# The tail of a fused attention and adapter kernel: who adds x to the last chunks, where the range count stands, and which queue carries the last store

## The chip, the cores and the metric

The kernel runs on one core of a Trainium2 chip. The metric is the device time of one execution in microseconds, and lower is better. Runs of the kernel before: 378.57, 376.80 and 375.92 us, median 376.8. One more execution was taken with the hardware profiler; its views are what the text quotes, in microseconds from the start of its span. The engines are called TensorE (PE; its weight loads are PEld), VectorE (DVE), ScalarE (ACT), GpSimd (POOL) and SyncE (SP, which issues most transfers).

## What is computed

Two layers behind each other. First attention of 49152 queries of width 128 (four batches of 12288) over 768 keys for each batch, which are pooled 4 x 4 from `kv` and multiplied by `w_sr`; keys and values are the same. Then, for each of the 49152 rows x, a mixture of two out of eight low-rank adapters:

```python
# attention, for each batch
kv_pool = kv.reshape(B, H // r, r, W // r, r, C).mean(axis=(2, 4))
k = v = kv_pool.reshape(B, -1, C) @ w_sr
a = softmax(q @ k.T / sqrt(C))
x = a @ v
# adapters, for each row of x
logits = x @ w_gate
topk = the two largest of 8
w = softmax(those two)
out = x + sum(w[e] * (x @ A[e]) @ B[e] for e in topk)
```

## The kernel before, in words

The 49152 rows go in 96 chunks of 512 tokens (four sub-blocks of 128 partitions, the "slots"). n is the number of the last chunk, 95. For each chunk TensorE makes the scores (L326), ScalarE their exponential (L327), TensorE the weighted values with the sum of the weights in an extra column (L338), and VectorE divides by that sum (L345 and L349, or L821 and L822 for the last two chunks), which gives x; the largest gate values are taken on VectorE (L356, L827). The gate's arithmetic runs on GpSimd (L365 to L369, or `gate_args` at L762 to L765, and `gate_w` at L775 and L776), its tanh on ScalarE (L768).

The adapters of a chunk then take these steps, each a function of the kernel: x is turned by TensorE and evicted (`turn`, L790 and L796 or L798); TensorE multiplies by all A (`hidden`, L806); VectorE multiplies by the gate (`gated`, L781); the gated rows are turned again (`turn`); TensorE multiplies by B (`up`, L486) into a PSUM bank; then x is added and the 256 KB of the chunk are stored (`put`, L505).

For the addition of x there are three ways. `add_rows` (L500): VectorE adds x to the PSUM bank and writes the output tile. `take` and `add` (L491, L495): ScalarE copies the bank into the output tile, and GpSimd, which cannot read PSUM, adds x there. `x_first` (L478): TensorE puts x into the bank by a float32 product with the identity, ahead of `up`, and ScalarE copies the sum out; no addition is left. Before the change n-7, n-3 and n-1 go by VectorE, n-6, n-5 and n-4 by ScalarE and GpSimd, and n-2 by TensorE. The last chunk is split: its first two slots go by TensorE (L892, L898) and ScalarE (L900), the other two by VectorE (L904).

The kernel leaves the maximum out of its softmax, and so checks that the sums lay in a safe range. `tail_ok` compares the last 15 chunks' reciprocals with two limits on GpSimd (L571, L572) and multiplies both (L573); `all_ok` counts on TensorE by a product with ones (L577) and makes a flag on VectorE (L578, L580). All five engines load the flag (L910) and branch (L913); if it is set, the whole is computed again by a slow path, which does not happen here.

The order is written out by hand: instructions stand on each engine in the order of the code, and an engine takes them strictly one behind the other. The stores of the tail are all issued from SP, also in the order of the code. The output tiles come from a pool of three buffers with room for two chunks each; the PSUM banks of the tail are named (`bank`, `fbank`, `t_bank`, `mtile`) and reused.

Of the kernel before, what the change touches and what calls it, by code (L numbers as in the profile page):

```python
# [16 lines left out]
ALU = mybir.AluOpType  # L17
# [4 lines left out]
def kernel(  # L22
# [10 lines left out]
    nc = tc.nc  # L33
    P = 128
    B, N, C = q.tensor.shape
# [5 lines left out]
    NTOK = 512  # L41
# [27 lines left out]
    def mtile(shape, dtype=FP32, name="hd"):  # L69
        return ps_h.tile(shape, dtype, tag="hd", name=name)  # L70
# [377 lines left out]
    def as_tokens(bank):  # L448
        return bank.rearrange("p (s c) -> p s c", s=NS)
# [21 lines left out]

    dps = {}

    def x_first(c, bank):

        dps[c] = as_tokens(bank)
        for s in range(NS):
            mm(dps[c][:, s], id_f32, xn[c][:, s, 0:C], start=(s == 0), stop=False,  # L478
               skip_group_check=True)

    def up(c, bank=None):
        fresh = c not in dps
        if fresh:
            dps[c] = mtile([P, NS, P], name="d_ps") if bank is None else as_tokens(bank)
        for s in range(NS):
            mm(dps[c][:, s], columns(hgT[c], c, s), b_bf, start=(s == 0 and fresh),  # L486
               stop=(s == NS - 1), skip_group_check=True)

    def take(c, lo=0, hi=NS):
        osb = half_out()  # L490
        nc.scalar.activation(osb[:, lo:hi], dps[c][:, lo:hi], AF.Copy)  # L491
        return osb

    def add(c, osb, eng):
        eng.tensor_tensor(osb, osb, xn[c][:, :, 0:C], op=ALU.add)  # L495

    def add_rows(c, lo=0, hi=NS, osb=None, bank_=None):
        osb = half_out() if osb is None else osb
        d = dps[c][:, lo:hi] if bank_ is None else bank_
        nc.vector.tensor_tensor(osb[:, lo:hi], d, xn[c][:, lo:hi, 0:C], op=ALU.add)  # L500
        return osb

    def put(c, osb, lo=0, hi=NS, queue=None):
        t0 = c * NTOK
        (queue or nc.sync).dma_start(  # L505
            out[t0:t0 + NTOK, :].rearrange("(p s) c -> p s c", p=P)[:, lo:hi], osb[:, lo:hi])
# [63 lines left out]
    def tail_ok():  # L570
        nc.gpsimd.tensor_scalar(ok[:, tail], rv[:, tail], 1.0 / L_HI, None, op0=ALU.is_ge)  # L571
        nc.gpsimd.tensor_scalar(low, rv[:, tail], 1.0 / L_LO, None, op0=ALU.is_le)  # L572
        nc.gpsimd.tensor_tensor(low, low, ok[:, tail], op=ALU.mult)  # L573

    def all_ok(bank):
        n = (NCH - CUT) * NS
        mm(bank[0:1, 0:n], ones_c, low, start=True, stop=True)  # L577
        nc.vector.tensor_reduce(last, bank[0:1, 0:n], axis=AX.X, op=ALU.add)  # L578
        full = float(P * NCH * NS + P * 2 * B + 2 * B)
        nc.vector.tensor_scalar(bad, last, tot, full, op0=ALU.add, op1=ALU.not_equal)  # L580


# [171 lines left out]
    def bank(i):  # L754
        return ps_e.tile([P, NTOK], FP32, tag=f"e{i}", name=f"e{i}")
# [22 lines left out]
    def gated(c, lo, hi, g, hb):  # L778
        if c not in hg:
            new_hg(c)  # L780
        nc.vector.tensor_tensor(  # L781
            hg[c][:, lo:hi].rearrange("p s (r e) -> p s r e", e=E),
            hb.rearrange("p s (r e) -> p s r e", e=E),
            g[:, lo:hi].unsqueeze(2).broadcast_to([P, hi - lo, RK, E]), op=ALU.mult)

    def turn(src, lo, hi, bank_, store, key, act=True):

        t_ps = bank_.bitcast(BF16)[:, 0:(hi - lo) * P].rearrange("p (s c) -> p s c", c=P)
        for s in range(lo, hi):
            mm(t_ps[:, s - lo], src[:, s], id_bf, is_transpose=True,  # L790
               start=(s == lo), stop=(s == hi - 1), skip_group_check=True)
        if key not in store:
            x_or_h = ("xt", 7) if store is xT else ("ht", 4)
            store[key] = run.tile([P, NS, P], BF16, tag=x_or_h[0], name="xr", bufs=x_or_h[1])
        if act:
            nc.scalar.activation(store[key][:, lo:hi], t_ps, AF.Copy)  # L796
        else:
            nc.vector.tensor_copy(store[key][:, lo:hi], t_ps)  # L798

    def high(c):  # L800
        return xn[c].bitcast(U16)[:, :, 1:2 * C:2].bitcast(BF16)
# [16 lines left out]
    def tops4(c, top, y):  # L818
        ri = rinv_all[:, c]
        xv = y[:, :, 0:2 * VW].rearrange("p b (s v) -> p b s v", v=VW)  # L820
        nc.vector.reciprocal(ri.rearrange("p (b s) -> p b s", b=2), xv[:, :, :, VW - 1])  # L821
        nc.vector.tensor_tensor(  # L822
            xn[c][:, :, 0:C + G].rearrange("p (b s) v -> p b s v", b=2), xv[:, :, :, 0:C + G],
            ri.rearrange("p (b s) -> p b s", b=2).unsqueeze(3).broadcast_to([P, 2, 2, C + G]),
            op=ALU.mult)
        for s in range(NS):
            nc.vector.max(top[:, s], xn[c][:, s, C:C + E])  # L827
# [13 lines left out]
    def fbank(i):  # L841
        return ps_f.tile([P, NTOK], FP32, tag=f"f{i}", name=f"f{i}")
# [6 lines left out]
    o6 = take(n - 6)  # L849
    h2 = hidden(n - 3, 0, NS, mtile([P, NTOK], name="h2"))  # L850
    up(n - 5, bank(0))
    o0 = take(n - 5)
    gate_args(n - 1, 0, NS, nc.gpsimd, top4, arg4, msk4)
    y5 = ps_e.tile([P, 2, 512], FP32, tag="y5", name="y5")
    weigh(n, 0, y5)
    gated(n - 3, 0, NS, gw[q_ - 1][:, 0:NS], h2)
    turn(high(n - 1), 0, NS, bank(1), xT, n - 1)
    h3 = hidden(n - 2, 0, NS, t_bank())
    gated(n - 2, 0, NS, gw[q_ - 1][:, NS:2 * NS], h3)
# [3 lines left out]
    o1 = take(n - 4)  # L863
    gate_w(0, NS, nc.gpsimd, arg4, msk4)
    tops4(n, top5, y5)
    turn(hg[n - 3], 0, NS, mtile([P, NTOK], name="t2"), hgT, n - 3)
    h4 = hidden(n - 1, 0, NS, bank(1))
    turn(hg[n - 2], 0, NS, t_bank(), hgT, n - 2)
    x_first(n - 2, fbank(0))
    turn(high(n), 0, NS, bank(0), xT, n)  # L870
    add(n - 6, o6, nc.gpsimd)
    put(n - 6, o6)
    gate_args(n, 0, NS, nc.gpsimd, top5, arg5, msk5)
    gate_tanh(0, NS, arg5)
    up(n - 3, mtile([P, NTOK], name="d2"))
    gated(n - 1, 0, NS, arg4, h4)
    put(n - 3, add_rows(n - 3))
    up(n - 2)
    o3 = take(n - 2)
    gate_w(0, NS, nc.gpsimd, arg5, msk5)  # L880
    x3 = ps_e.tile([P, 2, 512], FP32, tag="y5", name="x3")
    h5 = hidden(n, 0, NS, x3[:, 0])
    gated(n, 0, NS, arg5, h5)
    put(n - 2, o3)
    for c, o in ((n - 5, o0), (n - 4, o1)):
        add(c, o, nc.gpsimd)
        put(c, o)
    tail_ok()
    turn(hg[n - 1], 0, NS, bank(1), hgT, n - 1)
    d5 = as_tokens(fbank(1))  # L890
    for s in range(2):
        mm(d5[:, s], id_f32, xn[n][:, s, 0:C], start=(s == 0), stop=False, skip_group_check=True)  # L892
    turn(hg[n], 0, 2, bank(0), hgT, n)
    turn(hg[n], 2, 4, t_bank(), hgT, n, False)
    up(n - 1, mtile([P, NTOK], name="d4"))
    put(n - 1, add_rows(n - 1))
    for s in range(2):
        mm(d5[:, s], hgT[n][:, s], b_bf, start=False, stop=(s == 1), skip_group_check=True)  # L898
    o5 = half_out()
    nc.scalar.activation(o5[:, 0:2], d5[:, 0:2], AF.Copy)  # L900
    d6 = as_tokens(fbank(0))
    for s in range(2, 4):
        mm(d6[:, s - 2], hgT[n][:, s], b_bf, start=(s == 2), stop=(s == 3), skip_group_check=True)
    nc.vector.tensor_tensor(o5[:, 2:4], d6[:, 0:2], xn[n][:, 2:4, 0:C], op=ALU.add)  # L904
    put(n, o5)
    all_ok(bank(1))

    end_banks.close()
    ps_g = ctx.enter_context(tc.tile_pool(name="ps_g", bufs=1, space=bass.MemoryType.PSUM))
# [124 lines left out]
```

## Time and profile before

| what | us |
|---|---|
| median of three runs | 376.8 |
| the profiled execution, its own time | 375.43 |
| its span | 373.6 |
| TensorE busy | 356.5 |
| ScalarE busy | 309.4 |
| VectorE busy | 299.6 |
| GpSimd busy | 225.6 |
| last exponential ends on ScalarE | about 354 |
| the flag is written on VectorE | 370.14 |

How to read the lines of the prediction: a row of the timeline gives start, length, engine and line, the operation, what is written and read, the shapes, and in brackets the engine's idle time ahead of it with what ended it. A row of the chain gives start, length and what, of the one chain of work that ended last. In the strip of the DMA engines each digit is the busy share of a slice in tenths; the strip has 40 slices of the stretch named ahead of it.

### The profile page before, as it was taken

The page shows a single profiled execution, that of the slowest core. Times are in us where ns is not written, and L with a number is a line of the kernel's source. Part 1 is how long each engine was busy: PE and PEld are TensorE (multiplying, and loading weights), DVE is VectorE, ACT ScalarE, POOL GpSimd, SP SyncE. Part 2 cuts the span into 40 slices and gives each one's busy share as a digit, 9 for nine tenths or more (in the row PEclk, how much of TensorE's full clock was granted, in tenths as well). Part 3 has the DMA queues.
Part 4 walks back from the last instruction along what each step waited for, and adds up shares of the span by engine and source line. Part 5 has one row for each costly group of instructions (what it writes and reads, how often), then busy time and mean ns, then how long its engine had stood idle before and what let it go on. Part 6 is the DMA issues. An engine that isn't in the chain of part 4 may idle for free.

```text
span 373.6 us, 10589 instructions
## 1 busy us (share of the span) xinstructions
PE 356.5 (95%) x3942; PEld 262.8 (70%) x3943; DVE 299.6 (80%) x952; ACT 309.4 (83%) x391; POOL 225.6 (60%) x376
## 2 busy tenths in 40 slices
PE   4789999999999999999999999999999999999983
PEld 2456777777777677777777777777776767667772
DVE  3784558888888788888888888888888898998983
ACT  1579999989889798898898898898888888888862
POOL 1013799988799897755679697755444234232255
PEclk9999999999999999999999999999999999999998
DMA  8998999999999999999999999998789799663325
GB/s 261 413 360 218 316 300 304 298 318 306 286 335 320 308 292 331 226 317 314 304 288 361 303 313 317 253 302 260 227 225 257 206 255 245 184 145 131 130 86 201
DMA packets 95594, 101.01 MB, mean 270 GB/s; under 512 B 58804, under 2 KB 59060, under 8 KB 95540
## 3 DMA queue, kind: packets, MB, share of 16 engines
q1 hardware_dynamic: 94068, 100.11, 94.6%
q8 instruction: 31, 0.51, 0.6%
q10 hardware_dynamic: 1472, 0.20, 0.3%
q14 instruction: 23, 0.19, 0.2%
HBM read 62.33 MB, written 25.90 MB: 236 GB/s over the span
## 4 chain that ended last, share of the span: by engine, by line
PE 83%; DVE 5%; POOL 4%; DMA 3%; ACT 2%; issue 1%; SPq 0%; POOLq 0%; DVEq 0%
PE xps L338 33%; PE sg L326 30%; PE t_ps L405 5%; PE d_ps L486 5%; PE h_ps L440 4%; DMA kvt<-in_kv_dram 2%; DMA ge<-g_h 2%; ACT tt L327 1%; PE v_ps L215 1%; POOL osb L495 1%; DVE xn_all L349 1%; DVE osb L500 1%; DVE ht L443 1%; DVE kvt L191 1%; PE k_ps L240 1%
## 5 line engine op out<-in xcount | busy, mean ns | idle before, releaser
L327 ACT ACTIVATE tt<-sg 128x1024 f16<-128x1024 f32 x288 | 276.9, 1023 | 36.3 <-PE sg L326 35.5
L326 PE MATMUL sg<-qT,kfT 128*128 128x512 f16 x576 | 170.2, 379 | 0.5 <-ACT qT L593 0.3
L338 PEld LDWEIGHTS <-tt 128*128 128x128 f16 x2304 | 146.1, 98 | 28.4 <-DVE xn_all L349 18.1
L338 PE MATMUL xps<-vext,tt 128*128 128x136 f16 x2256 | 164.7, 223 | 0.3 <-DVE xn_all L349 0.2
L500 DVE TENSOR_TENSOR osb<-d_ps,xn_all 128x512 f32<-128x512 f32 x85 | 58.7, 691 | 28.7 <-PE d_ps L486 27.7
L365 POOL TENSOR_TENSOR arg<-xn_all,top 128x64 f32<-128x64 f32 x47 | 14.5, 308 | 99.6 <-DVE top L356 80.2
L349 DVE TENSOR_TENSOR xn_all<-xps,rinv_all 128x540 f32<-128x540 f32 x94 | 67.7, 721 | 3.3
L326 PEld LDWEIGHTS <-kfT 128*128 128x128 f16 x576 | 49.1, 98 | 24.4 <-issue 1.5
L191 POOL TENSOR_TENSOR kvt<-kvt 128x1024 f32<-128x1024 f32 x27 | 63.7, 2361 | 2.1 <-PE t_ps L405 2.0
L107 POOL CAST q<-q 128x1024 f16<-128x1024 f32 x45 | 46.8, 1042 | 24.0 <-DMA q<-in_q_dram 24.0
L443 DVE SCALAR_TENSOR_TENSOR ht<-ge,h_ps 128x512 bf16<-128x512 f16 x87 | 58.5, 673 | 1.4 <-DMA ge<-g_h 1.0
L486 PEld LDWEIGHTS <-ht 128*128 128x128 bf16 x368 | 27.0, 98 | 24.6 <-DVE ht L443 5.7
L356 DVE MAX8 top<-xn_all 128x8 f32<-128x8 f32 x376 | 35.1, 156 | 6.3
L416 DVE COPY xt<-t_ps 128x512 bf16<-128x512 bf16 x92 | 36.8, 400 | 0.0
L405 PE MATMUL t_ps<-id_bf,xn_all 128*128 128x128 bf16 x376 | 36.3, 219 | 0.0
L486 PE MATMUL d_ps<-b_bf,ht 128*128 128x128 bf16 x340 | 32.9, 219 | 0.8 <-DVE ht L443 0.7
L440 PE MATMUL h_ps<-xt,a_bf 128*128 128x512 bf16 x86 | 32.6, 379 | 0.1
L345 DVE RECIPROCAL rinv_all<-xps 128x4 f32<-128x4 f32 x94 | 17.1, 182 | 13.6 <-PE xps L338 12.2
L405 PEld LDWEIGHTS <-xn_all 128*128 128x128 bf16 x376 | 25.9, 98 | 0.3
L368 POOL TENSOR_SCALAR msk<-msk 128x64 f32<-128x64 f32 x47 | 20.2, 429 | 4.1
L369 POOL TENSOR_TENSOR arg<-arg,msk 128x64 f32<-128x64 f32 x47 | 15.1, 321 | 3.9
L367 POOL TENSOR_TENSOR arg<-arg,msk 128x64 f32<-128x64 f32 x47 | 15.1, 320 | 3.7
(150 smaller groups left out, 221.0 us busy)
## 6 DMA issues: line engine op xcount, KB each, us to landing
kvt<-in_kv_dram SPq DMA_DIRECT2D x48, 512.0 KB
q<-in_q_dram SPq DMA_DIRECT2D x46, 512.0 KB
out_dram<-osb SPq DMA_DIRECT2D x44, 512.0 KB
ge<-g_h SPq DMA_DIRECT2D x45, 256.0 KB
out_dram<-osb SPq DMA_DIRECT2D x8, 256.0 KB
q<-in_q_dram SPq DMA_DIRECT2D x1, 1024.0 KB
qT<-q SPq DMA_TRANSPOSE x46
g_h<-g_sb SPq DMA_DIRECT2D x45, 16.0 KB
```

The lines of the kernel that those rows point to most:

```text
L107: nc.gpsimd.tensor_copy(q16[i], q32[i].rearrange("p k n -> p (k n)"))
L191: eng.tensor_tensor(v[:, 0], v[:, 0], v[:, d], op=ALU.add)
L326: mm(sg[:, k], kfT[b][:, j * P:(j + 1) * P], qc, start=True, stop=True)
L327: nc.scalar.activation(tt[c][:, 2 * r:2 * r + 2], sg, AF.Exp, bias=0.0, scale=scale)
L338: mm(o, tt[c][:, j, s * P:(s + 1) * P], vext[b][:, j, 0:VW], start=(j == 0 and s % 2 == 0), stop=(j == NJ - 1 and s % 2 == 1), skip_group_ ...
L349: nc.vector.tensor_tensor(xn[c][:, :, 0:C + G].rearrange("p (b s) v -> p b s v", b=2), xv[:, :, :, 0:C + G], ri.rearrange("p (b s) -> p b ...
L405: mm(columns(t_ps, c, s), src[:, s], id_bf, is_transpose=True, start=(s == 0), stop=(s == NS - 1), skip_group_check=True)
L416: nc.vector.tensor_copy(to, t_ps)
L440: mm(h_ps, a_bf, xT[c], start=True, stop=True)
L443: nc.vector.scalar_tensor_tensor(hgT[c].rearrange("p (k a) t -> p k (a t)", k=2), gE[c // 2][:, h:h + NS // 2].rearrange("p a t k -> p k ( ...
L486: mm(dps[c][:, s], columns(hgT[c], c, s), b_bf, start=(s == 0 and fresh), stop=(s == NS - 1), skip_group_check=True)
L500: nc.vector.tensor_tensor(osb[:, lo:hi], d, xn[c][:, lo:hi, 0:C], op=ALU.add)
```

## The change

All of it is in the tail, from L471 on; the loop over the chunks stays.

- n-5: VectorE adds x from PSUM (`add_rows`); ScalarE's copy and GpSimd's addition go.
- n-6: its addition on GpSimd moves ahead of the gate weights of n-1, and its store behind that of n-5.
- n-2: VectorE adds x; TensorE's eight float32 products with the identity and ScalarE's copy go.
- n-1: TensorE puts x under it (`x_first`, now callable for some slots, in two halves) and ScalarE copies; VectorE's addition goes.
- n-4: still ScalarE and GpSimd, its addition now behind the gate weights of n.
- The range tests move ahead of the gate of n, and the product of the two comparisons goes: TensorE counts both, and the expected count is larger by that number.
- Count and flag move from behind the last store to behind the last turning of n.
- The float32 products of the first half of n write another bank (the second of the tile that holds the hidden rows of n) and stand behind `up(n - 1)`.
- The last store is issued from ScalarE's queue.

```diff
-    def x_first(c, bank):
-        dps[c] = as_tokens(bank)
-        for s in range(NS):
+    def x_first(c, bank, lo, hi):
+        dps[c] = as_tokens(bank) if lo == 0 else dps[c]
+        for s in range(lo, hi):
...
     def tail_ok():
...
-        nc.gpsimd.tensor_tensor(low, low, ok[:, tail], op=ALU.mult)
...
-        mm(bank[0:1, 0:n], ones_c, low, start=True, stop=True)
+        mm(bank[0:1, 0:n], ones_c, ok[:, tail], start=True, stop=False)
+        mm(bank[0:1, 0:n], ones_c, low, start=False, stop=True)
...
-        full = float(P * NCH * NS + P * 2 * B + 2 * B)
+        full = float(P * (NCH * NS + n) + P * 2 * B + 2 * B)
...
     up(n - 5, bank(0))
-    o0 = take(n - 5)
...
     gated(n - 3, 0, NS, gw[q_ - 1][:, 0:NS], h2)
+    put(n - 5, add_rows(n - 5))
+    add(n - 6, o6, nc.gpsimd)
+    put(n - 6, o6)
...
     gate_w(0, NS, nc.gpsimd, arg4, msk4)
     tops4(n, top5, y5)
+    tail_ok()
...
     turn(hg[n - 2], 0, NS, t_bank(), hgT, n - 2)
-    x_first(n - 2, fbank(0))
     turn(high(n), 0, NS, bank(0), xT, n)
-    add(n - 6, o6, nc.gpsimd)
-    put(n - 6, o6)
...
     up(n - 3, mtile([P, NTOK], name="d2"))
+    x_first(n - 1, fbank(1), 0, 2)
     gated(n - 1, 0, NS, arg4, h4)
+    up(n - 2, fbank(0))
     put(n - 3, add_rows(n - 3))
-    up(n - 2)
-    o3 = take(n - 2)
-    gate_w(0, NS, nc.gpsimd, arg5, msk5)
+    put(n - 2, add_rows(n - 2))
     x3 = ps_e.tile([P, 2, 512], FP32, tag="y5", name="x3")
     h5 = hidden(n, 0, NS, x3[:, 0])
+    turn(hg[n - 1], 0, NS, bank(1), hgT, n - 1)
+    gate_w(0, NS, nc.gpsimd, arg5, msk5)
     gated(n, 0, NS, arg5, h5)
-    put(n - 2, o3)
-    for c, o in ((n - 5, o0), (n - 4, o1)):
-        add(c, o, nc.gpsimd)
-        put(c, o)
-    tail_ok()
-    turn(hg[n - 1], 0, NS, bank(1), hgT, n - 1)
-    d5 = as_tokens(fbank(1))
+    x_first(n - 1, fbank(1), 2, 4)
+    up(n - 1)
+    o4 = take(n - 1)
+    put(n - 1, o4)
+    add(n - 4, o1, nc.gpsimd)
+    put(n - 4, o1)
+    d5 = as_tokens(x3[:, 1])
     for s in range(2):
         mm(d5[:, s], id_f32, xn[n][:, s, 0:C], start=(s == 0), stop=False, skip_group_check=True)
     turn(hg[n], 0, 2, bank(0), hgT, n)
     turn(hg[n], 2, 4, t_bank(), hgT, n, False)
-    up(n - 1, mtile([P, NTOK], name="d4"))
-    put(n - 1, add_rows(n - 1))
+    all_ok(bank(1))
...
-    d6 = as_tokens(fbank(0))
+    d6 = as_tokens(mtile([P, NTOK], name="d6"))
...
-    put(n, o5)
-    all_ok(bank(1))
+    put(n, o5, queue=nc.scalar)
```

## The prediction

> **What bounds the kernel now.** I read the page's first part and its chain first: they say what the body is bound by, and so whether an edit of the tail can matter.
>
> ```profile
> span 373.6 us, 10589 instructions
> PE 83%; DVE 5%; POOL 4%; DMA 3%; ACT 2%; issue 1%; SPq 0%; POOLq 0%; DVEq 0%
> ```
>
> TensorE carries 83% of the chain, but the order of the changed program differs from that of the old one only after the last exponential, from about 358 us on. So the body keeps its time, and I look only at the last 15 us. There the chain in order of time is another one (columns: start, length, what):
>
> ```profile
> 362.60 0.25 POOL r L776
> 362.86 1.22 POOL osb L495
> ...
> 365.85 2.44 POOL osb L495 x2
> 368.29 0.33 POOL ok L571
> 368.62 0.33 POOL low L572
> ...
> 369.03 0.32 POOL low L573
> ...
> 369.39 0.28 PE e L577 x2
> ...
> 369.70 0.22 DVE last L578
> ...
> 369.94 0.20 DVE bad L580
> ```
>
> GpSimd ends last: behind the last gate (ending at 365.85) it adds two chunks (2.44), runs the range tests, and only then TensorE counts and VectorE writes the flag, at 370.14.
>
> What follows the flag comes from the rows of the flag's load (L910) and of the program's end (L1029):
>
> ```profile
> L910 SPq TENSOR_LOAD <-bad x1: 869/869/869, 370.2 to 370.2; - x1
> ```
>
> ```profile
> L1029 SPq EVENT_SEMAPHORE x10: 17/28/28, 372.3 to 373.6; - x10
> L1029 SPq DRAIN x3: 7/7/13, 372.8 to 373.1; - x3
> ```
>
> From the flag's end to the end of the span are 373.6 - 370.1 = 3.5 us of load, branch, semaphore checks and barrier, all fixed. SP starts its closing checks at 372.3 and runs through them without a gap. A second path ends there too, that of the stores (the SP rows, then the busy tenths of the DMA engines, the first strip from 358.75 in steps of 0.05 us, the second from 369.25 in steps of 0.1 us):
>
> ```profile
> 358.75 0.34 SPq L505 DMA_DIRECT2D out_dram<-osb  x1
> ```
>
> ```profile
> DMA  0000000000000000169898997989966300000000
> ```
>
> ```profile
> 369.28 0.37 SPq L505 DMA_DIRECT2D out_dram<-osb  x1
> ```
>
> ```profile
> DMA  9999999999999998999721000000022003000000
> ```
>
> A store that finds the DMA engines empty is moved 1.6 us after its issue (358.75 to 360.35). The last store, issued at 369.28 into a queue that is full, is mostly moved by 371.25 and has stragglers until 371.5. It is not late, but it is not far from being so: SP's checks come about 0.8 us behind it.
>
> **The change part by part.** These rows of the timeline carry the terms (start, length, engine and line; in brackets the engine's idle time before):
>
> ```profile
> 361.65 0.69 DVE L781 TENSOR_TENSOR hgs<-t_ps,th 128x512 bf16<-128x512 f32 x1 [1.00 <-PE t_ps L806]
> ...
> 362.22 0.29 POOL L775 TENSOR_SCALAR r<-r 128x32 f32<-128x32 f32 x1 [0.91 <-ACT r L768]
> ...
> 362.81 1.27 POOL L495 TENSOR_TENSOR osb<-osb,xn_all 128x512 f32<-128x512 f32 x1
> ...
> 363.05 1.11 PE L478 MATMUL f<-xn_all,id_f 128*128 128x128 f32 x8
> ...
> 363.33 0.37 DVE L827 MAX8 top<-xn_all 128x8 f32<-128x8 f32 x4
> ...
> 364.00 0.39 PE L790 MATMUL e<-id_bf,xn_all 128*128 128x128 bf16 x4
> ...
> 364.04 0.24 POOL L762 TENSOR_TENSOR r<-xn_all,top 128x32 f32<-128x32 f32 x1
> ...
> 364.65 0.69 DVE L500 TENSOR_TENSOR osb<-d,xn_all 128x512 f32<-128x512 f32 x1 [0.35 <-PE d L486]
> ...
> 365.22 0.29 POOL L775 TENSOR_SCALAR r<-r 128x32 f32<-128x32 f32 x1
> ...
> 365.53 0.66 PE L892 MATMUL f<-xn_all,id_f 128*128 128x128 f32 x4
> ...
> 365.60 0.25 POOL L776 TENSOR_TENSOR r<-r,r 128x32 f32<-128x32 f32 x1
> 365.79 0.60 ACT L796 ACTIVATE xr<-e 128x512 bf16<-128x512 bf16 x1 [0.17 <-PE e L790]
> ...
> 365.88 0.69 DVE L781 TENSOR_TENSOR hgs<-x,r 128x512 bf16<-128x512 f32 x1 [0.54 <-POOL r L776]
> ...
> 366.63 0.28 PE L790 MATMUL e<-id_bf,hgs 128*128 128x128 bf16 x2 [0.44 <-DVE hgs L781]
> ...
> 367.01 0.38 ACT L796 ACTIVATE xr<-e 128x256 bf16<-128x256 bf16 x1 [0.62 <-PE e L790]
> 367.14 0.29 DVE L798 COPY xr<-t_ps 128x256 bf16<-128x256 bf16 x1 [0.56 <-PE t_ps L790]
> ...
> 367.94 0.41 DVE L904 TENSOR_TENSOR osb<-f,xn_all 128x256 f32<-128x256 f32 x1
> ```
>
> 1. *Chunk n-5 from GpSimd to VectorE.* 0.69 us on VectorE, placed ahead of the 361.65 row, which has 1.00 idle before it: covered, cost nothing. Its ScalarE eviction goes. Were the idle time not there, the gating of n-2 and all behind it would slip by up to 0.69.
> 2. *Chunk n-6 earlier on GpSimd.* 1.27 us goes ahead of the 362.22 row, into 0.91 of idle time: the weights of n-1 come 1.27 - 0.91 = 0.36 later, at 362.85 + 0.36 = 363.21. Their reader, the gating of n-1, stands on VectorE behind the maxima of the last chunk, which end at 363.33 + 0.37 = 363.70; so the 0.36 is covered, with 0.49 to spare.
> 3. *Range tests, without the product, ahead of the gate of n.* 2 x 0.33 from the chain's rows: 363.21 + 0.66 = 363.87, against 364.04 now, because the add that stood there has gone. The last gate's weights are ready 0.17 earlier: 365.85 - 0.17 = 365.68.
> 4. *x under n-2 on TensorE goes (8 matmuls, 1.11), VectorE adds n-2 instead.* The turning of x of n at 364.00 may go up to 0.7 earlier and the product of n-3 with it, so VectorE's add of 364.65 moves to about 364.3; the new add (0.69) follows it and ends at 365.68, in the 0.54 of idle time and the 0.35 gained. Gating of n: 365.72 instead of 365.88, ending at 366.41. This cover is exact: each tenth that the add of n-3 does not gain puts the gating back by the same tenth.
> 5. *x under n-1 (two halves of 4 matmuls).* They lie where TensorE waits: ahead of the product of n-2, and behind the turning of n-1. ScalarE's eviction of that turning, now at 365.79, loses its take of n-2 ahead of it and comes near 365.4; the product of n-1 is done by 366.4. GpSimd's and VectorE's adds for it are gone; ScalarE takes 0.6 instead, before it is needed for the last turning.
> 6. *x under the first half of n.* Now 4 matmuls at 365.53, off the path. In the new order they write the second bank of the tile whose first bank the gating of n reads, and the built program lets them wait for that gating. They stand ahead of the last turning, so this is a new cost on the path: eight such took 364.00 - 363.05 = 0.95 until the next group, four 0.48. Last turning: 366.41 + 0.06 + 0.48 = 366.95 against 366.63, 0.32 later.
> 7. *Count and flag.* VectorE's copy of the turning moves by the same 0.32 and ends at 367.75. TensorE counts meanwhile (two products where the chain has one of 0.28; 367.2 to about 367.6). Sum and compare take 370.14 - 369.70 = 0.44: flag at 368.20 against 370.14, 1.94 us earlier. The product on GpSimd (0.32) is gone.
> 8. *The last store.* VectorE's last add (0.41) stands behind the flag: 368.20 to 368.62, against 368.35 now. But there the store still stood behind four others on SP until 369.28; on ScalarE's queue it issues near 368.70, 0.58 earlier. SP's seven stores go out earlier too (n-5 and n-6 by 362.7, n-3, n-2, n-1 between 365 and 367.5, n-4 when GpSimd's add ends, 365.68 + 1.27 = 366.95, behind n-1). Behind the issue on ScalarE only its own flag load is queued, so it loads about 0.9 later than SP; SP's checks come 2.1 us after its load began, which covers it.
>
> The price of a store on ScalarE's queue is not in the tail. The nearest rows are the first load there and its reader:
>
> ```profile
> 0.74 0.40 ACTq L138 DMA_DIRECT2D w_in<-in_w_sr_dram  x1
> ```
>
> ```profile
> 2.79 0.23 DVE L155 TENSOR_SCALAR w_sr_sb<-w_in 128x128 f32<-128x128 f32 x1 [1.93 <-DMA w_in<-in_w_sr_dram]
> ```
>
> Issue 0.40 against 0.34, and 2.05 us from issue to its reader for 64 KB. So the last store (256 KB) is moved 1.6 us after issue if the engines are empty, or, as the one at 369.28, in 2.3 us if they are not: 370.3 to 371.0. From the moved data to the end of the span lies at least 0.85 (SP's first closing drain at 372.8 to 373.65) and at most 2.1 (371.5 to 373.6). I take 1.3, between them and nearer the lower, since SP went through its checks unhindered: 371.6 to 372.3.
>
> **Sum.** Flag path: 368.20 + 3.5 = 371.7. Store path: 371.6 to 372.3, middle 372.0. The later decides: span 372.0, a gain of 1.6 us. The profiled execution took 375.43 us by its own time, 1.8 outside the span; it becomes 373.8. It lies 1.4 under the median of the runs (376.8), so the median becomes 375.2.
>
> By the Trainium skill ("DMA: Bandwidth & Descriptors", Anatomy of one DMA, which speaks of the GpSimd path) a transfer costs about 2.0 us fixed, most of it the receipt of the last write, plus its bytes over 436 GB/s. That makes an estimate of 2.6 us here, a landing at 371.3 and an end near 372.2, so the store and not the flag would decide; the 64 KB load (2.05 seen, 2.15 by the rule) agrees.
>
> **Rivals.**
> *The stores decide by more.* Moving the adds earlier leaves the same eight stores of 256 KB for sixteen DMA engines, and the strip shows one or two engines late (the 1, the 2 after 371.2). If one engine is a store or two behind, the last one is moved near 371.5 as now, less one store's 0.6: span 372.6 to 373.2, gain 0.4 to 1.0, median 376.1. For it: the stragglers. Against: two of the eight now leave before 363.
> *Nothing is gained.* The late turning (step 6) grows: if the add of n-2 holds the gating of n by another 0.7 and the x half by its whole 0.66, flag at 369.1 and last store at 369.6, moved by 371.9. Span 373.4, median 376.6. For it: the cover of step 4 has no reserve. Against: 365.68 on both engines.
> *Slower.* ScalarE's queue has carried nothing since the start. The second load there reached its reader later than the first:
>
> ```profile
> 1.17 0.45 ACTq L140 DMA_DIRECT2D w_gate_sb<-in_moe_w_gate_dram  x1
> ```
>
> ```profile
> 5.36 0.56 PE L165 MATMUL wg_ps<-w_gate_sb,wT 128*128 128x8 f32 x2 [1.74 <-DMA w_gate_sb<-in_moe_w_gate_dram]
> ```
>
> That is 4.19 us from issue to reader. The last store makes the kernel slower from 373.65 - 0.85 - 368.7 = 4.1 us after issue on. At 4.19 the span is 373.7; with the upper bound of what follows, 2.1 behind data moved at 372.3, it is 374.4: median 376.9 to 377.6. For it: a queue this long unused. Against: the 2.05 of the first load, on a queue equally unused, and that the second load's 4 KB go in rows of 32 bytes, which the store's do not.
> *Only the flag counts.* Store moved at 370.3 and receipt short: span 371.7 or, without step 6's wait, 371.3; median 374.5 to 374.9.
>
> **How the numbers follow.** Forecast (gain 1.2 to 2.0) 0.58, stores by more 0.18, flag alone 0.08, nothing 0.09, slower 0.07. The runs before spread from 375.92 to 378.57, and the profiled one was at 375.43; the forecast's own range is 375.43 - 2.0 = 373.4 to 376.8 - 1.2 = 375.6. With the two rivals of smaller gain, and half a microsecond for the runs, 373.5 to 377.1 holds 8 in 10. One per cent, 3.8 us, is about what a measurement of this kernel can tell from no change. No case gains that: the whole stretch from the last gate to the flag is 4.3 us, of which the turnings stay. So faster 0.04 and slower 0.03, both for the spread of the runs and the tail of the ScalarE case, same 0.93.
>
> **What would show it.** Right: GpSimd's last add ends near 367.0 with no range test behind it; the flag near 368.2; VectorE with three adds at 128x512 after 361; TensorE's last turning near 366.95 behind the four float matmuls; a store on ScalarE's queue near 368.7. Wrong: a gap of SP in its closing checks of more than 0.5 us (the store decides), the gating of n after 366.0 (step 4 or 3), the last store's data after 371.2, or a body longer than now ahead of 358 us.

## The result and the profile after

| | before | after |
|---|---|---|
| median of 20 runs, us | 375.89 (375.28 to 380.62) | 374.75 (373.77 to 376.81) |
| ratio, 95% interval | | 0.9957 [0.9940, 0.9973] |
| the profiled execution, us | 375.43 | 374.92 |
| its span | 373.6 | 373.0 |

The time falls by 1.1 us of 376, within the one per cent that the prediction called no change; it had 375.2. The first part and the chain of the page of after:

```profile
span 373.0 us, 10593 instructions
PE 84%; DMA 7%; DVE 5%; ACT 1%; issue 1%; SPq 1%; POOL 1%; ACTq 0%; DVEq 0%
```

GpSimd's share of the chain fell from 4% to 1%. The two spans can't simply be subtracted. The first store that both programs issue at the same point of the work, that of n-7, stands at 358.75 in before and here:

```profile
359.85 0.34 SPq L505 DMA_DIRECT2D out_dram<-osb  x1
```

That is 1.1 us later. It is scatter of the body: in eight profiled executions of kernels with the new tail and an untouched body (after, E1 to E4, E6, E11, E12) this store is issued between 358.63 and 359.85, and in E5, which has the body of before, at 360.13. It arises at the start. ScalarE's waits ahead of the exponentials (L327) run in before and in after

```profile
L327 ACTq EVENT_SEMAPHORE  x92: 17/17/17, 32.2 to 350.6; - x92
```

```profile
L327 ACTq EVENT_SEMAPHORE  x92: 17/17/17, 33.3 to 351.7; - x92
```

which is 318.4 us from the first to the last in both: the 1.1 us are there by the first row and do not change any more. So the tails are compared from the issue of n-7 on, and I call that time z. The tail of before lasts from 358.75 to 373.65, 14.90 us; that of after from 359.85 to 373.03, 13.18: 1.72 less, where the prediction had 1.6.

The chain of after in order of time (start, length, what):

```profile
364.46 0.40 PE e L790 x4
...
365.22 0.50 PE f L478 x4
...
366.52 0.60 ACT xr L796
367.13 0.05 issue
367.17 0.40 PE f L486 x4
367.57 0.56 PE x L894 x4
368.13 0.13 PE e L790 x2
...
368.34 0.39 ACT xr L796
...
368.78 0.29 PE x L899 x2
369.06 0.13 PE d L904 x2
...
369.21 0.42 DVE osb L905
```

The late additions and the range tests on GpSimd (L495, L571 to L573), which carried before's chain from 362.9 to 369.4, are off it; the one late addition left on GpSimd (n-4) stands beside it. The chain now runs over TensorE and ScalarE, through the product of n-1 (L486) and x of the last chunk's first half (L894), to the last turning, and ends at the addition for the last store. The waits of SP from 366 us on say which path ends last (who waits, for whom, us in total, times, longest):

```profile
SPq L505 <- DVE osb L500: 2.3, 2, 1.9
...
SPq L1029 <- DMA out_dram<-osb: 0.5, 1, 0.5
```

The second line is the answer to "which path decides": SP's closing checks (L1029) stop for half a microsecond until a store has landed. Before had no such wait. By the trace's rows it lasts 0.56 us, from 371.51 to 372.07. So the flag has half a microsecond in hand.

The timeline rows for the prediction's steps (start, length, engine and line, operation):

```profile
361.67 0.68 DVE L500 TENSOR_TENSOR osb<-e,xn_all 128x512 f32<-128x512 f32 x1
362.75 0.69 DVE L781 TENSOR_TENSOR hgs<-t_ps,th 128x512 bf16<-128x512 f32 x1 [0.41 <-PE t_ps L806]
```

```profile
363.98 0.25 POOL L776 TENSOR_TENSOR r<-r,r 128x32 f32<-128x32 f32 x1
...
364.52 0.36 POOL L572 TENSOR_SCALAR low<-rinv_all 128x60 f32<-128x60 f32 x1
364.65 0.60 ACT L796 ACTIVATE xr<-t_ps 128x512 bf16<-128x512 bf16 x1
...
365.31 0.68 DVE L500 TENSOR_TENSOR osb<-d,xn_all 128x512 f32<-128x512 f32 x1
365.98 0.69 DVE L500 TENSOR_TENSOR osb<-f,xn_all 128x512 f32<-128x512 f32 x1
...
366.39 0.25 POOL L776 TENSOR_TENSOR r<-r,r 128x32 f32<-128x32 f32 x1
...
366.60 1.26 POOL L495 TENSOR_TENSOR osb<-osb,xn_all 128x512 f32<-128x512 f32 x1
366.68 0.69 DVE L781 TENSOR_TENSOR hgs<-x,r 128x512 bf16<-128x512 f32 x1
...
367.42 0.71 PE L894 MATMUL x<-xn_all,id_f 128*128 128x128 f32 x4
...
367.97 0.27 PE L790 MATMUL e<-id_bf,hgs 128*128 128x128 bf16 x2
...
368.94 0.20 DVE L580 TENSOR_SCALAR bad<-last,tot 1x1 int32<-1x1 f32 x1
...
369.72 0.38 ACTq L505 DMA_DIRECT2D out_dram<-osb  x1
```

And the DMA engines of after, from 366 us in steps of 0.1:

```profile
DMA  0000000838899988989898601000013799999999
...
q8 instruction: 1, 0.02, 2.1%
```

There are two things here that the prediction's sum did not have. The stores of n-3 and n-2 are moved from 366.7 to 368.2, and behind them about one engine of the sixteen is still at work (digits of 0 and 1). And in the same stretch falls one 16 KB packet on queue 8: the DMA engines also bring TensorE's next instructions.

### The profile page after: what moved, and what is told of

It is laid out like the page before. It is cut to its first block, busy times and chain, and to the rows that moved or that the text cites. A ratio compares the mean times of both kernels' runs of the same rounds, so it can differ in the third digit from the quotient of the medians.

```text
span 373.0 us, 10593 instructions
## 1 busy us (share of the span) xinstructions
PE 358.1 (96%) x3945; PEld 263.0 (70%) x3945; DVE 300.2 (80%) x953; ACT 308.7 (83%) x390; POOL 223.5 (60%) x374
## 4 chain that ended last, share of the span: by engine, by line
PE 84%; DMA 7%; DVE 5%; ACT 1%; issue 1%; SPq 1%; POOL 1%; ACTq 0%; DVEq 0%
PE xps L338 34%; PE sg L326 30%; PE t_ps L405 5%; PE d_ps L486 5%; PE h_ps L440 5%; DMA b_f<-in_moe_B_dram 3%; DMA kvt<-in_kv_dram 2%; DMA ge<-g_h 2%; PE v_ps L215 1%; ACT tt L327 1%; DVE xn_all L349 1%; DVE osb L500 1%; DVE ht L443 1%; SPq L87 1%; PE kp_ps L207 0%
## 5 line engine op out<-in xcount | busy, mean ns | idle before, releaser
L327 ACT ACTIVATE tt<-sg 128x1024 f16<-128x1024 f32 x288 | 276.8, 1022 | 37.2 <-PE sg L326 36.5
L486 PEld LDWEIGHTS <-ht 128*128 128x128 bf16 x368 | 26.9, 98 | 24.8 <-DVE ht L443 6.1
L486 PE MATMUL d_ps<-b_bf,ht 128*128 128x128 bf16 x340 | 32.9, 219 | 0.7 <-DVE ht L443 0.7
```

What stands on the lines that cost most here:

```text
L327: nc.scalar.activation(tt[c][:, 2 * r:2 * r + 2], sg, AF.Exp, bias=0.0, scale=scale)
```

## The experiments

The prediction's account, theory A: the new division of the additions lets both paths to the end come forward; x of the last half waits (step 6), and the last store, not the flag, decides by a few tenths. Its rivals: one part alone (the flag, or ScalarE's queue) carries the gain; or the stores are held back by something else than their issue. The last became theory C after E4: it is the load of TensorE's instructions that makes one DMA engine late, and that engine sets the end. Each expectation states what it holds against what; that of E1 names theory C, since it was written after the results of E2 to E5.

All in us from z; each line is one profiled execution, the ratios are from 7 to 12 timed runs (after: 20) against before. "Landed" is when 15 of the 16 engines, and when the last one, reported the last store done.

| kernel | last turning | flag | last store issued | landed, 15 / 16 | end | ratio, 95% interval |
|---|---|---|---|---|---|---|
| before | 7.88 | 11.39 | 10.53 | 12.96 / 13.39 | 14.90 | |
| after | 8.12 | 9.29 | 9.87 | 11.94 / 12.21 | 13.18 | 0.9957 [0.9940, 0.9973] |
| E1 after again | 8.11 | 9.28 | 9.86 | 11.95 / 12.42 | 13.39 | |
| E2 last store on SP | 8.11 | 9.28 | 9.87 | 12.90 / 13.15 | 14.12 | 0.9953 [0.9932, 0.9975] |
| E3 flag last | 8.12 | 10.14 | 9.87 | 11.93 / 12.18 | 13.22 | 0.9959 [0.9934, 0.9985] |
| E4 x early | 7.65 | 8.82 | 9.71 | 12.50 / 12.63 | 13.61 | 0.9955 [0.9931, 0.9980] |
| E5 before, flag early | 7.87 | 9.27 | 11.15 | 14.09 / 14.55 | 15.52 | 1.0025 [0.9995, 1.0054] |
| E6 x and count aside | 7.57 | 7.86 | 9.62 | 12.79 / 12.90 | 13.87 | 0.9967 [0.9954, 0.9980] |
| E7 load moved | 8.11 | 9.28 | 9.86 | 11.94 / 12.08 | 13.05 | 0.9977 [0.9958, 0.9996] |
| E8 = E6 with E7 | 7.57 | 7.86 | 9.62 | 11.93 / 13.65 | 14.63 | 1.0021 [1.0006, 1.0036] |
| E9 load clear of all | 8.11 | 9.28 | 9.86 | 11.92 / 11.95 | 12.92 | 0.9989 [0.9965, 1.0013] |
| E10 all aside, load clear | 7.57 | 7.86 | 9.33 | 11.57 / 12.02 | 13.00 | 0.9979 [0.9955, 1.0004] |
| E11 = E10, old start | 7.57 | 7.86 | 9.33 | 12.12 / 12.24 | 13.22 | 0.9971 [0.9951, 0.9992] |
| E12 adds alone | 8.12 | 10.13 | 9.87 | 12.22 / 12.81 | 13.78 | 0.9955 [0.9939, 0.9971] |

**E1, the changed kernel again.** Nothing edited.

> The changed kernel, unaltered, profiled once more, to see how far the tail's length repeats. Theory C, formed from the runs so far (16 KB of TensorE's instructions are loaded in the midst of the last stores, by one of the sixteen DMA engines, which is then behind for all later stores, and by more or less from run to run): the engines' own steps repeat to 0.05 (last turning 8.1, flag 9.3, last store issued 9.9 after the store of n-7), while the landing of the last store and with it the tail moves by some tenths, 13.1 to 13.7. Rival (the tail repeats as a whole): 13.2, within 0.05.

The engines' steps repeat to 0.01; the landing of the last store moved by 0.2, and with it the end (13.39 against 13.18). So a difference of a step is read to hundredths, one of the end only to some tenths.

**E2, the last store on SP.**

```diff
-    put(n, o5, queue=nc.scalar)
+    put(n, o5)
```

> The changed kernel with one thing undone: the last store is issued from SP again. Measure for this and the other runs: the tail, from the issue of the store of n-7 to the end of the span (14.9 us in the kernel before, 13.2 in the changed one), because the body's own spread is larger than the effects. Theory A (the landing of the last store ends the tail, SP waits for it 0.5 us in its closing checks, the flag has that much in hand): SP's flag load starts only behind the issue, at about 0.95 later than now, uses up the 0.5 and becomes the end itself: tail 13.6, no gap left in SP's checks. Rival B (the queue does not matter, what counts is the moment VectorE's last add ends): tail 13.2.

The time does not change against after (0.9953), and neither of the two tails expected (13.6, 13.2) came: it is 14.12. SP issues the store at z + 9.87, no later than ScalarE did. In this profiled execution the stores land later, but that begins before the edited place: the third of the late stores, that of n-1, occupies SP for 0.89 us where it took 0.33 in after.

```profile
367.68 0.89 SPq L505 DMA_DIRECT2D out_dram<-osb  x1
```

Before shows such a long issue, too, at 367.10 (0.81), for its third late store, that of n-5. So ScalarE's queue brings no earlier issue; the issue came forward because SP has nothing left to wait for when VectorE's last addition is done.

**E3, the flag behind the last store again.**

```diff
-    all_ok(bank(1))
...
     put(n, o5, queue=nc.scalar)
+    all_ok(bank(1))
```

> The changed kernel with count and flag put back behind the last store; the adds and the queue stay as changed. Theory A (the store decides, the flag has 0.5 us in hand): the flag comes about 1.0 later, half of it is absorbed, tail 13.6 to 13.7. Rival B (the flag decides already in the changed kernel): the whole 1.0 is lost, tail 14.2.

The flag comes 0.85 later and the end does not move (13.22, ratio 0.9959). The half microsecond of SP's wait for the store is used up, as its waits show: there is one for the flag (L910) and none for a store any more.

```profile
SPq L910 <- DVE bad L580: 1.0, 1, 1.0
SPq L1029 <- PEq L1029: 0.6, 2, 0.5
```

I had expected the end to come some tenths later. From the flag to the end it took 3.08 us here against 3.51 in before: the stretch that the prediction called fixed is not. SP's load of the flag took 0.76 us in after and 0.48 here (0.87 in before; why it differs was not tried):

```profile
L910 SPq TENSOR_LOAD <-bad x1: 761/761/761, 369.2 to 369.2; - x1
```

```profile
L910 SPq TENSOR_LOAD <-bad x1: 480/480/480, 369.0 to 369.0; - x1
```

So of the 0.85 by which the flag is later, the load gives back 0.28, and SP's wait of 0.56 holds the rest.

**E4, x of the last half ahead of its wait.** The two products go into a bank that is free earlier, ahead of `up(n - 1)`.

```diff
+    d5 = as_tokens(fbank(0))
+    for s in range(2):
+        mm(d5[:, s], id_f32, xn[n][:, s, 0:C], start=(s == 0), stop=False, skip_group_check=True)
     up(n - 1)
...
-    d5 = as_tokens(x3[:, 1])
-    for s in range(2):
-        mm(d5[:, s], id_f32, xn[n][:, s, 0:C], start=(s == 0), stop=False, skip_group_check=True)
```

> The changed kernel, with the x of the first half of n put into the bank that n-2 has left, ahead of the product of n-1, so that it does not wait for the gating of n. Theory A (these four float32 products are a new 0.5 us on the path to the last turning, and the last store behind it ends the tail): the turning of the gated rows of n starts 0.35 after the gating ends minus what the product of n-1 takes, near 0.25 behind it instead of 0.6; everything behind moves by 0.35, tail 12.8. Rival B (TensorE waits there for the eviction of the turning of n-1 anyway, the products are hidden): tail 13.2.

The last turning is at 366.98, z + 7.65, 0.47 earlier: the wait of step 6 is real and its size right. But the end did not follow (13.61; ratio 0.9955). The last store is issued only 0.16 earlier and lands later, at 12.63, and SP waits for stores:

```profile
SPq L1029 <- DMA out_dram<-osb: 0.8, 2, 0.6
```

So here the end did not come from the turning. With all that E2 showed this led to theory C.

**E5, before with an early flag.** In before, `tail_ok()` (in its new form) goes ahead of the loop that adds n-5 and n-4, and the count behind `up(n - 1)`.

```diff
+    tail_ok()
     for c, o in ((n - 5, o0), (n - 4, o1)):
         add(c, o, nc.gpsimd)
         put(c, o)
-    tail_ok()
...
     up(n - 1, mtile([P, NTOK], name="d4"))
+    all_ok(bank(1))
...
     put(n, o5)
-    all_ok(bank(1))
```

> The kernel before with the early flag alone: range tests (two comparisons, no product) ahead of the last two adds on GpSimd, count and flag behind the last turning; who adds x to which chunk and the queue of the last store stay as before. Theory A (flag and stores are two paths that end close together): the flag comes near 368.0, but the two adds slip by 0.66, the last store is issued near 369.9 and decides: tail 14.8 to 15.0, no gain against 14.9. Rival B (the late flag alone was the loss): flag at 368.0 plus 3.5, tail 12.7.

The flag is as early as in after (9.27), and nothing is gained: tail 15.52, ratio 1.0025. The tests go ahead of GpSimd's additions, these move back, and SP waits for them in its stores; its own load of the flag stands behind them at z + 11.69, 2.4 behind the flag.

```profile
SPq L505 <- POOL osb L495: 2.4, 2, 1.6
...
SPq L1029 <- DMA out_dram<-osb: 0.5, 1, 0.5
```

An early flag is worth nothing without the new division of the additions.

**E6, x and the count aside.** The turnings of n go ahead of x of its first half, and the count goes ahead of `up(n - 1)` into a bank of its own.

```diff
+    all_ok(mtile([P, NTOK], name="cnt"))
     up(n - 1)
...
+    turn(hg[n], 0, 2, bank(0), hgT, n)
+    turn(hg[n], 2, 4, t_bank(), hgT, n, False)
     d5 = as_tokens(x3[:, 1])
...
-    turn(hg[n], 0, 2, bank(0), hgT, n)
-    turn(hg[n], 2, 4, t_bank(), hgT, n, False)
-    all_ok(bank(1))
```

> The changed kernel with two things taken out of the way of the last turning: the x of the first half of n stands behind that turning, and count and flag stand ahead of it, in a bank that is free by then. By the engines' rows the last turning comes 0.5 earlier (7.6 after the store of n-7), the flag near 8.0, the last store is issued near 9.4. If the engines' path ends the tail: 12.6 to 12.7. By theory C (the DMA engine that is behind sets the landing, whatever the engines do): the store lands no earlier than 12.2 and the tail is 13.1 or more, although its issue is 0.5 earlier.

The flag is 1.43 earlier, the turning 0.55, the last store's issue only 0.25, since ScalarE's copy of n-1 (0.60), which stood ahead of its copy of the turning before, too, now ends after the turning and holds that copy up. The end is later (13.87): again n-1's issue takes 0.88, and the stores land late. It is not one engine alone: the last store, issued 0.27 behind that of n-4, has landed on fourteen engines only at 12.32, 2.70 behind its issue, and on the other two at 12.79 and 12.90. So theory C's one late engine does not tell the whole of this run.

```profile
SPq L505 <- ACT xr L796: 1.4, 1, 1.4
SPq L1029 <- DMA out_dram<-osb: 0.9, 2, 0.6
```

**E7, the load of instructions moved.** The page of after has the loads in its part on queues (packets, MB, share):

```profile
q8 instruction: 31, 0.51, 0.6%
```

That is 16 KB each, one for some 254 of TensorE's 3945 matmuls and 3945 weight loads. A start with 124 more TensorE instructions shifts it: half of the 18 warming products (`warm`, products at the start whose result nobody reads) are replaced by 71 products of one column, whose result nobody reads either.

```diff
-    warm(18)
+    warm(9)
+    tiny = mtile([P, 1], name="tiny")
+    for i in range(71):
+        mm(tiny, id_bf, id_bf[:, 0:1], start=True, stop=True)
```

> The changed kernel; at the start, nine of the 18 warming products are replaced by 71 one-column products, so that TensorE's program is 124 instructions longer ahead of the tail and the load of its last 16 KB of instructions falls 4 to 5 us earlier, between the stores of n-7 and n-5. The start of the kernel may shift by some tenths, the tail's engines' steps do not. Theory C: no DMA engine is behind at the last store, it lands about 2.05 after its issue instead of 2.34, SP's wait shrinks from 0.56 to about 0.25, tail 12.8 to 12.9. Rival (the stragglers come from the stores' own density): 13.2.

The load went from z + 6.9 to z + 2.5. The store of n-3 now lands at 8.17 with 15 engines and 8.20 with the last (after: 8.19 and 9.72), those of n-2, n-1 and n-4 within 0.04, and the end is at 13.05 (12.8 to 12.9 expected). It is the store of n-5, the one just issued when the load starts, that now has a late engine (landed at 4.53 and 5.10). In the strip of the DMA engines (from 368 in steps of 0.1) nothing straggles behind the first pair of stores:

```profile
DMA  8899998989899610000000999899898999971399
```

That is theory C's evidence by removal. The ratio is 0.9977, no better than after's: z was at 360.99, so the altered start cost the body what the tail gained, or more.

**E8, E6 and E7 together.**

> Both: count, flag and x aside of the last turning, and the instruction load moved. Theory C with the engines' path: last store issued near 9.4, landed at 11.45; SP's flag load stands behind its own issue for n-4 and starts near 9.2; tail 12.4 to 12.6, against 13.2, and the time 0.6 us under that of the changed kernel, if the altered start costs nothing. Rival: the tail stays at 12.9 or more, because something else holds the landing.

This was meant to be the best version and became the second slowest. The four late stores ahead of the last land together. But in E7, too, a further load of 16 KB comes at the jump behind the flag, at z + 11.77, when the last store is all but landed; with the early flag TensorE jumps earlier, and the load is at z + 10.87, in the midst of that store. In both runs it starts 1.2 us behind the end of TensorE's branch (z + 10.59 and 9.64). Fifteen engines had it done at 11.93, one at 13.65, and SP waited 2.1 us for it:

```profile
SPq L1032 <- DMA out_dram<-osb: 2.1, 1, 2.1
```

```profile
DMA  9899999898999898305002000101010010000000
...
q8 instruction: 1, 0.02, 2.0%
```

The strip (from 370 in steps of 0.1) shows that one engine, its work trickling in until 373.3. That is theory C's evidence by addition: the same load behind the store's issue costs the end 1.6 us against E7, and the time shows it (1.0021).

**E9, the load clear of all late stores.** As E7, with 13 warming products and 33 of one column (56 more instructions).

> The changed kernel with five of the 18 warming products at the start replaced by 33 one-column products: TensorE's program is 56 instructions longer ahead of the tail, so the load of its last 16 KB of instructions should fall about 4.5 us after the store of n-7, between the stores of n-6 and n-3, and the next one behind the end. In the run that moved it by 124 instructions, a further load came with the jump at the end and met the last store. Theory C (the load alone makes one DMA engine late): all sixteen engines land every store from n-3 on within 0.1 us, the last store lands about 2.1 after its issue at 9.87, tail 12.9 to 13.0 against 13.2 to 13.4. Rival (the stragglers have another cause): first and last landing of the stores stay 1.5 us apart.

The load is at z + 4.2, and the late engine has gone with it: the store of n-6 lands at 5.81 with fifteen engines and at 7.12 with the last. All five late stores land on the last engine within 0.04 of the fifteenth, the last store at 11.95, 2.09 behind its issue, the shortest tail of all (12.92). In the strip from 371 nothing of the store is left behind its 3 at 373.2 (three small loads of instructions, 8 KB each, make the 5 and the 2), and SP's wait is 0.3:

```profile
DMA  8999999989999615898999305000200000000000
```

```profile
SPq L1032 <- DMA out_dram<-osb: 0.3, 1, 0.3
```

Against after's 13.18 the late engine is thus worth 0.26, against E1's 13.39 it is 0.47. The time does not show it (0.9989): z was at 361.77. The body lost that in its middle, not at its start: the waits at L327 run from 32.5 to 353.6, 321.1 us against 318.4, and over the whole run VectorE waits longer for the gate values of the chunks (`ge`) to be loaded, E9 first, then after:

```profile
DVE ht L443 <- DMA ge<-g_h: 4.1, 5, 1.7
```

```profile
DVE ht L443 <- DMA ge<-g_h: 1.1, 2, 0.9
```

**E10 and E11, all aside.** E6 with ScalarE's copy of n-1 behind the turnings of n and the store of n-4 ahead of it; E10 with E9's start, E11 with the old one.

```diff
+    all_ok(mtile([P, NTOK], name="cnt"))
     up(n - 1)
-    o4 = take(n - 1)
-    put(n - 1, o4)
     add(n - 4, o1, nc.gpsimd)
     put(n - 4, o1)
+    turn(hg[n], 0, 2, bank(0), hgT, n)
+    turn(hg[n], 2, 4, t_bank(), hgT, n, False)
+    o4 = take(n - 1)
+    put(n - 1, o4)
...
-    turn(hg[n], 0, 2, bank(0), hgT, n)
-    turn(hg[n], 2, 4, t_bank(), hgT, n, False)
-    all_ok(bank(1))
```

> The changed kernel with count, flag and x of n's first half out of the way of the last turning, ScalarE's copy of n-1 behind its copy of that turning, the store of n-4 ahead of that of n-1, and the instruction load moved by 56 instructions. Engines: last turning 7.6, its copy on ScalarE starts near 7.9 instead of 8.5, last store issued near 9.3 instead of 9.9. Theory C: landed near 11.4, SP's own closing path (flag load near 9.35, behind the issue for n-1) is then as late: tail 12.6 to 12.8, 0.5 under the changed kernel, time ratio to the kernel before 0.994. Rival: the landing stays at 12.0 or later because four stores stand too close, tail 13.0 or more.

> The same as the run with everything aside, but with the 18 warming products of the changed kernel, so that the instruction load falls among the last stores again. Theory C: the engines' steps are those of that run (last store issued near 9.3), but one DMA engine is behind, and the store lands at 12.1 to 12.9: tail 13.1 to 13.9. Rival (the engines' path decides): tail 12.6 to 12.8.

The last store is issued at 9.33, 0.54 earlier than in after. E10 has fifteen engines done at 11.57 but one at 12.02, and ends at 13.00, no earlier than E9; expected were 12.6 to 12.8, and its rival's numbers (landed at 12.0 or later, tail 13.0 or more) are the ones that came. Three small loads of instructions (8 KB each, queue 14) lie in that stretch; whether they are the cause, or the stores standing too close, as the rival says, was not tried. By the landings, one engine is 0.45 behind the others there, and so is a second engine in E4, E6 and E11 (0.44 to 0.47). E11, with the load at z + 7.1 among the stores, lands at 12.24 and ends at 13.22: of the 0.54 nothing is left. Neither beats the changed kernel (0.9979 and 0.9971).

**E12, the additions alone.** E2 and E3 together: queue and flag as in before, only the division and the early range tests new.

> The changed kernel without its last two parts: count and flag stand behind the last store again, and that store is issued from SP. What is left is the new division of the adds, with the range tests ahead of the last gate. If GpSimd's late adds were the loss (they held the stores and, through the range tests, the flag), the gain stays: flag near 10.1, last store issued at 9.9, both 0.6 to 1.3 earlier than before, tail 13.5 to 14.1 according to the instruction load, ratio 0.995 to 0.998. Rival (the early flag or ScalarE's queue is needed): tail 14.5 or more, ratio 0.999 or more.

Ratio 0.9955, the whole gain. The profiled tail is 13.78, 0.6 longer than after's, with n-1's issue at 0.79; the timed runs, whose interval is some 0.6 us either way, show none of it.

## Why the prediction was right

With 1.1 subtracted, after's rows stand on the prediction's time.

*Steps 1 and 2.* VectorE's addition of n-5 (0.68) ends ahead of the gating of n-2, whose row at 362.75 becomes 361.65, the very place it had: covered, with 0.41 of idle time left. The weights of n-1 are ready at 363.98 + 0.25, which is 363.13 (363.21).

*Step 3.* The range tests end at 364.52 + 0.36, which is 363.78 (predicted 363.87); the last weights are ready at 366.64, which is 365.54 (365.68).

*Step 4.* The additions of n-3 and n-2 stand back to back and end at 366.67, which is 365.57 (365.68); the gating of n follows and ends at 366.27 (366.41). The cover without reserve held: VectorE has no idle time between the three rows.

*Step 5.* Right in its times: ScalarE's copy of the turning of n-1 starts at 366.52, which is 365.42 (365.4), the product of n-1 ends at 367.57, which is 366.47 (366.4), and ScalarE's copy of n-1 (367.61) ends before that of the last turning starts (368.34). That both halves of x under n-1 lie where TensorE waited is right only in part: the first half is on the chain (365.22), and without it the product of n-2 at 365.56 would have waited only for ScalarE's copy, which ends at 365.25. By the rows it cost nothing at the last turning, since x of n waits for the gating of n, until 367.37, in any case.

*Step 6.* Right: the four products put 0.55 ahead of the last turning (0.48), which is at 366.87 (366.95), 0.24 later than before, and E4 and E6, which take the wait away, bring it 0.47 and 0.55 earlier.

*Step 7.* The flag is at 368.04 (368.20), 2.10 earlier. That it is worth little was in the sum (the store decides), and E3 and E5 show it. "All fixed" for the 3.5 us behind it was wrong: 3.51 in before, 3.08 in E3.

*Step 8.* The issue is at 368.62 (368.70), the landing 2.07 to 2.34 behind it, the end at 371.93 (372.0). The moment was right, the reason half wrong: I credited ScalarE's queue with the 0.58, reckoning with before's queue on SP. E2 and E12 have the same issue at 9.87 on SP. Nor did the flag hold VectorE's last addition, as the sum has it: in E3, where no flag stands ahead of it, the store is issued at 9.87 as well. What removed the wait there was the new division, which lets the store of n-4 go earlier. The rest of the path has its size: the last store's data are moved by about 371.7, which is 370.6 (370.3 to 371.0), and 1.3 us are left to the end, as the sum had put it between two bounds. The strip of after from 369 in steps of 0.1 shows that store from the 7 at 370.6 on (the last digits are also three loads of instructions):

```profile
DMA  3799999999999960799999921322000000000000
```

*The deciding path.* I forecast the store, 0.3 behind the flag path; SP's wait is 0.56, just over the 0.5 above which I had called the forecast wrong: that the store decides by so much did not cost the forecast its sum, because the flag path was shorter than 3.5. A second sign of being wrong, a longer body ahead of 358 us, also appeared in this execution; it is the scatter of the start shown above. Of the rivals, "the stores decide by more" had seen the right stragglers, but put them down to too many stores in a queue; E7, E8 and E9 show that it is the load of instructions. "Slower" is excluded: the store on ScalarE's queue landed at most 2.34 behind its issue in after, not 4.1 (only in E8, with the load in its midst, was it 4.04). "Nothing" is excluded by the interval. "Only the flag counts" has the measured median in its range (374.5 to 374.9); against it stand SP's wait for the store and E3, where the flag comes 0.85 later and the end stays. Two rivals' spans do not follow from their own terms: with the sum's 1.3 us, "nothing" comes to 371.9 + 1.3 = 373.2 instead of 373.4, and "the stores decide by more" to 371.5 - 0.6 + 1.3 = 372.2, within the forecast's range, instead of 372.6 to 373.2.

*The gain.* Tails: 1.72, or 1.51 with E1 (predicted 1.6). Medians: 1.1; the ratio gives 1.6, with an interval of 1.0 to 2.3. That the median itself, 374.75, comes so near the 375.2 is in part luck: the forecast started from 376.8, the median of three runs, where twenty have 375.89; from there 1.6 less is 374.3.

The Trainium skill ("DMA: Bandwidth & Descriptors", Anatomy of one DMA) gave an estimate of 2.6 for the last store. Undisturbed it took 2.09 (E9), and the store of n-7 2.03: the measurement decides, and the page's figure, which is for GpSimd's path, is 0.5 too long for stores from ScalarE and SP. On instructions, the Trainium skill ("Runtime: NRT & Kernel Launch", Instruction fetch mechanics) has blocks of 16 KiB for 256 instructions, which the trace bears out, and calls their cost mostly hidden. What such a load costs in the body was not tried; among the last stores it is not hidden, as E8 shows with 1.7 us on one engine.

What stays open: which of the moved additions carries the gain (n-5, n-2 and n-1 were not tried one by one) and how much the early range tests add to it, and why the altered start made the body longer (z at 360.35 to 361.77 in E7 to E10, against 358.63 to 359.85). Where it did is known: E7 and E8 are late at the first row of L327 (34.1 and 33.6) and take 318.7 and 318.6 us from there to its last, E9 and E10 take 321.1 and 320.6, with VectorE waiting 4.1 and 3.6 us for `ge`. A version that beats the changed kernel was not found.

## What to carry to other kernels

When the end hangs on one engine's additions, divide them over the engines by their idle time just there; moving the flag alone, or one store to another queue, gained nothing here. Two paths that end within half a microsecond of each other take turns: bringing one forward shows only as much as the other allows. When the engines' steps come earlier and the end does not, look at the last of the sixteen DMA engines, not at their mean.

## What the runs showed that I had not expected

- One 16 KB load of TensorE's instructions among the stores leaves one of sixteen DMA engines 1.2 to 2.2 us behind the others at the store of n-3 (E5: landed at 8.63 and 9.87; after: 8.19 and 9.72; E2: 8.20 and 10.41). Out of the way, all sixteen are within 0.04 for that store (E7, E9), and the lateness is at the store that the load now meets.
- With an engine so far behind, SP's issue of the third store takes 0.5 to 0.9 us instead of 0.33 (before, E2, E4, E6, E11, E12), and everything behind it on SP waits. In these six the issue ends 1.73 to 1.79 us before the last engine has landed the store ahead, so by these rows it is that engine that holds it.
- A store issued on ScalarE 0.27 behind one on SP (E6) landed 3.28 after its issue; issued 1.07 behind (after), 2.34. That two queues are the cause is not shown: in E2 the last store, on SP like the one 0.51 ahead of it, took 3.28 as well.
- Bringing the jump at the end forward brings its load of instructions forward too (from z + 11.77 in E7 to 10.87 in E8).
